# Earlier sends of turned blocks, one read back instead of three, later stores and a new VectorE price in a fused attention and feed-forward kernel

## The chip, the cores and the metric

The kernel runs on one core of one Trainium2 chip. The metric is the device time of one execution in microseconds (us); a measurement is the median of several executions. The core's engines are PE (matrix products; PEld is its weight load), DVE (VectorE), ACT (ScalarE), POOL (GpSimd) and SP (SyncE, which here only issues DMAs). Each engine works through its own instructions in program order and waits on semaphores for the others.

## What is computed

All in fp32, for 2048 tokens of 576 numbers, 32 heads of 18, and a hidden width of 4608:

```python
x = A_x
xn = _layernorm(x, axis=-1)
return x + _A_ref(xn, A_wqkv, A_wo) + _B_ref(xn, B_w1, B_w2)
```

`_A_ref` is attention in which a token looks at eight keys: itself and the tokens 2, 4, ... 14 before it; the result is multiplied by `wo`. `_B_ref` is `relu(xn @ w1) @ w2`. The kernel gets fp32 accuracy from a faster matmul format (fp32r) by splitting each operand into a high part and a rest (low part) and adding three products.

## The kernel before

**Phases and blocks.** The tokens are split by parity, since a step of 2 never leaves it: a phase (`ph`) holds the 1024 tokens of one parity as eight blocks of 128 (`i`), in pairs of 256 columns (`tb`). A phase runs over 12 chunks of w1/w2 (`c`), four `tb`, and three pieces of 128 hidden columns (`f`): 144 **slots** in a phase, 288 in all, numbered in that order (`slots`, L574). Slot n of the main loop (L867) has PE do half of a pair of first-layer products (`h_two`, L615, for slots two ahead; 14 pairs of matmuls in even slots, 13 in odd ones), then the second-layer products of the slot (`o_two`, L641). In odd slots ACT takes the relu into `hhi` and DVE makes the rest `hlo` (L597, L600). In slots with f = 2, `o_out` (L695) adds the four PSUM results into x on DVE (L709); in the last chunk the finished blocks are then stored by SP (L714). PSUM banks for the first layer alternate between two pools, except near q, k, v work, when only two banks serve, so that `h_two` of an even slot waits for `hlo` of the slot before.

**Attention** comes in four units of eight heads per phase. Eight slots in a row (7 to 14, 31 to 38, 55 to 62, 79 to 86 of a phase) also have the q, k, v products of one unit (`qkv_tile`, L406), which makes a slot 5.7 us instead of 3.1. The rest is DVE work, queued by `attention` (L449) in the slot after the unit's last block: products with the keys (`qk_mul`, L465), their sums (`qk_sum`, L468; after the last one POOL puts the mask in, L471), the softmax (`sm_max`, L477, to `sm_div`), products with the values (`av_mul`, L497) and their sums (`av_add`, L504).

**The plan.** While the program is written out, it keeps two estimated clocks, `t["pe"]` and `t["dve"]`. `dve(n)` (L133) prices a VectorE instruction of n elements at (n + 130) / 960 us. At the end of each slot `run_bg` (L522) takes pieces of attention from the queue as long as the DVE's clock with the next piece stays within `t["pe"] + margin(n)` (L859). So prices and margins decide in which slot each piece stands in DVE's program, and nothing else.

**wo.** In chunk 10, slots 122, 125, 128 and 131 of a phase (266, 269, ... in the second) also add the attention result times wo, two blocks each; such a slot lasts about 10 us. A block of attention output must be turned first: `wo_a` (L535) turns 32 x 32 tiles on DVE (L541, L542) into a tile `tr` (two buffers), `blocks_out` (L353) sends it to DRAM in four DMAs of 80 KB (L358), `wo_f` (L547) reads it back in one DMA of 320 KB with the blocks in place (L549; tile `xn`, three buffers), and `wo_s` (L551) splits it on ACT (L558) and DVE (L559, L560). The slots of these four steps come from `WO_STEPS`, counted from the block's slot: -5, -4, -3, -1 for even blocks and -4, -3, -2, -1 for odd ones.

**x of the second phase.** Its first four blocks go the same way between slots 126 and 143: load, `stats`, `norm_turned` (ACT), `xt_a` (turn, L373), `blocks_out`, `xt_f` (L377: three DMAs, one of 256 KB and two of 32 KB), `xt_s` (split, L391 to L395). `XT_STEPS` gives their slots, counted from 132. The normed block and its turned copy lie in one buffer of the attention products' pool `pr` (two buffers). The other four blocks are turned by PE. Slot 144 is the first whose `h_two` needs blocks 2 and 3.

**SP's queue.** SP issues in program order: within a slot first the staging loads of weights (`stage_more`, four splits ahead, five buffers `st`, so that a load waits for the split before the one it follows), then what `at` put there, then what `late` put there. A wait of SP for a transfer holds all later issues.

Of the kernel before, what the change touches and what calls it, by code (L numbers as in the profile page):

```python
# [10 lines left out]
F32 = mybir.dt.float32  # L11
# [7 lines left out]
P = 128  # L19
# [13 lines left out]
WO_CHUNK = 10  # L33

XT_STEPS = (
    (-6, 0, 1, 2, 3, 4, 7),
    (-5, 1, 2, 3, 4, 5, 8),
    (-3, 2, 3, 4, 5, 6, 10),
    (3, 4, 5, 6, 7, 8, 11),
)  # L40

WO_STEPS = ((-5, -4, -3, -1), (-4, -3, -2, -1))
HEADW = (-9, -8, -7, -6, -5, -4)
FIRST = 4

# [14 lines left out]
def tile_body(ctx: ExitStack, tc: tile.TileContext, x, wqkv, wo, w1, w2, out):  # L60
    nc = tc.nc
    S, D = x.shape
# [4 lines left out]
    NCH = NF // C  # L67
    KT = 4
    DR = D - KT * P
# [25 lines left out]
    turned = pool("turned", 4, space=bass.MemoryType.DRAM)  # L95
# [17 lines left out]
    o_v = out.rearrange("(p i two) d -> two i p d", i=NI, two=NPH)  # L113


    t = {"pe": 0.0, "dve": 0.0}
# [14 lines left out]
        return ins  # L131

    def dve(n):  # L133
        t["dve"] += (n + 130) / 960.0


    tasks = deque()
# [108 lines left out]
    X, XT, XN, MR = {}, {}, {}, {}  # L246
# [116 lines left out]
    def norm_turned(ph, i):  # L363
        nm, r = MR.pop((ph, i))
        z = prp.tile([P, W, UD], F32, name="pr").rearrange("p w c -> p (w c)")
        XN[ph, i] = xn, _ = z[:, 0:D], z[:, D : 2 * D]
        nc.scalar.activation(xn, X[ph, i], AF.Identity, bias=nm)
        nc.scalar.activation(xn, xn, AF.Copy, scale=r)

    def xt_a(ph, i):  # L370

        xn, tr = XN.pop((ph, i))
        nc.vector.transpose(tr, xn)  # L373
        dve(D)
        TD[ph, i] = turned.tile([D // 32, 32, P], F32, name="words"), tr

    def xt_f(ph, i):  # L377
        tb, h = divmod(i, 2)
        if h == 0:
            XT[ph, tb] = xtp.tile([P, 10, TBN], F32R, name="xT")  # L380
        z, td = f32(XT[ph, tb][:, 0:5, h * P : (h + 1) * P]), TD.pop((ph, i))[0]
        nc.sync.dma_start(z[:, 0:KT], td[0 : 4 * KT].rearrange("(k c) j i -> (c j) k i", k=KT))
        for rows in slice(0, DR), slice(DR, P):
            nc.sync.dma_start(z[rows, KT], td[4 * KT : D // 32].rearrange("c j i -> (c j) i"))

    def xt_s(ph, i):

# [11 lines left out]
    TD = {}  # L399
# [42 lines left out]
    bg = deque()  # L442
# [6 lines left out]
    def attention(ph, u):  # L449
        qo, k, v = QO[ph], KK[ph, u], VV[ph, u]  # L450
# [57 lines left out]
        n, big = NI * W * HG, W * UD  # L508
# [2 lines left out]
                for j in (i, i + 1):  # L511
                    bg.append((big, f, (j,)))
        for f in (sm_max, sm_sub, sm_exp, sm_sum, sm_rcp, sm_div):
            bg.append((0 if f is sm_exp else n + 130, f, ()))
        for i in range(0, NI, 2):
            for j in (i, i + 1):
                bg.append((big, av_mul, (j,)))
# [155 lines left out]
    def o_mm(n, out=True, which=range(2)):  # L673
# [18 lines left out]
        if out:  # L692
            o_out(n, which)

    def o_out(n, which=range(2), rows=False):  # L695
        ph, c, tb, f = slots[n]
        if f < C - 1:
            return
        end = n == len(slots) - 1
        t["dve"] = max(t["dve"], t["pe"] - 0.4)  # L700
        order = [(k, h) for k in which for h in range(2)]
        if rows:
            order.sort(key=lambda z: z[1])
        elif end:
            order.sort(key=lambda z: (z[0], -z[1]))
        for k, h in order:
            i = 2 * tb + k
            acc, cols = X[ph, i], CUT[h]
            nc.vector.tensor_tensor(acc[:, cols], PO[k, h], acc[:, cols], op=ALU.add)  # L709
            dve(cols.stop - cols.start)  # L710
            if end and k:
                (nc.scalar if h else nc.sync).dma_start(o_v[ph, i][:, cols], acc[:, cols])
            elif c == NCH - 1 and (k, h) in (order[-1], order[-2 if rows else 1]):
                nc.sync.dma_start(o_v[ph, i], acc)  # L714


    todo = {}
# [1 line left out]
    def at(n, f, *a):  # L719
        todo.setdefault(n, []).append((f, a))  # L720
# [3 lines left out]
    def late(n, f, *a):  # L724
        todo_late.setdefault(n, []).append((f, a))
# [3 lines left out]
    for ph in range(NPH):  # L729
# [7 lines left out]
        for u in range(NU):  # L737
            s = b + UNIT0 + u * UNIT_STEP
            plan.append((s - 5, wq_tasks, ((ph, u), u)))
            for i in range(NI):  # L740
                at(s + i, qkv_tile, ph, u, i)
                busy_m.add(s + i)
            late(s + NI + 1, attention, ph, u)
        plan.append((b + WO_CHUNK * SPC - 6, wo_tasks, (ph,)))
        for i in range(NI):
            z = b + WO_CHUNK * SPC + C * (i // 2) + C - 1
            turn, send, back, parts = (z + k for k in WO_STEPS[i % 2])
            late(turn, wo_a, ph, i)
            late(send, blocks_out, ph, i)
            (at if i % 2 else late)(back, wo_f, ph, i)  # L750
            at(parts, wo_s, ph, i)
        if ph + 1 < NPH:
            e = b + SPP - SPC
            for i in range(NI):
                if i >= len(XT_STEPS):
                    z = e + 3 + 2 * i - (i == NI - 1)
# [6 lines left out]
                load, first, second, turn, send, back, parts = (e + k for k in XT_STEPS[i])  # L763
# [77 lines left out]
    h4[0]()  # L841
    h4[1]()
    o_out(2, (0,))
    x4 = make_xt(0, 4, parts=True)
    for f in x4[:3]:
# [13 lines left out]
    def margin(n):  # L859

        odd, qkv = n % 2 == 0, n + 1 in busy_m
        due = sum(z[0] <= n + 1 for z in (*staged, *tasks))
        if slots[n][3] == 1:
            return (1.8 if odd else 2.7) + 2.4 * qkv - 0.8 * due
        return (2.5 if odd else 3.5) + 2.4 * qkv - 0.8 * due

    for n in range(FIRST, len(slots)):  # L867
        if n == ROW0:
# [47 lines left out]
```

## Time and profile before

| | us |
|---|---|
| time, median of 3 | 1172.0 (1169.96 to 1173.31) |
| the profiled execution's own time | 1171.2 |
| its span, first to last instruction | 1169.5 |
| PE busy in it | 1152.5 |
| DVE busy in it | 804.8 |
| mean granted clock of PE | 0.996 |

The span is what the trace covers; the profiled execution took 1.7 us more around it. All times of single instructions below are from that execution, in us from the start of the span. In rows of the timeline a merged group shows the start, the length and the count, and in brackets the idle time before it with what ended it. Rows of the waits show the sum, the number and the longest.

### The profile page before, as it was taken

What the parts mean: (1) busy time and instruction counts of PE and PEld (TensorE: products, weight loads), DVE (VectorE), ACT (ScalarE), POOL (GpSimd) and SP (SyncE); (2) the same over time, 40 slices, a digit from 0 to 9 for tenths busy, and PEclk for the clock granted to TensorE, in tenths of its full rate; (3) what the DMA queues carried; (4) which work ended last, traced back from release to release, by engine and by line L of the source; (5) the groups of instructions that cost most, each with busy time, mean ns of one, the idle gap of its engine ahead of it and who ended that gap; (6) DMA issues with size and microseconds to landing.
All of it is one profiled execution on the core that took longest, in us unless ns stands there. A gap on an engine that the chain in (4) does not pass through costs nothing.

```text
span 1169.5 us, 38344 instructions
## 1 busy us (share of the span) xinstructions
PE 1152.5 (99%) x17114; PEld 1142.7 (98%) x17114; DVE 804.8 (69%) x1457; ACT 287.7 (25%) x756; POOL 43.4 (4%) x60
## 2 busy tenths in 40 slices
PE   9999999999999999899999999999999999998998
PEld 8999999999999999899989999999999999998998
DVE  7428687878877888553663286977787878884533
ACT  5322222221222222121432122122222212221210
POOL 3200000000000000000010000000000000000000
PEclk9999999999999999999999999999999999999999
DMA  5312312311222212643552212122213222226502
GB/s 183 98 38 64 84 45 58 84 56 47 73 66 68 67 34 65 155 110 90 138 173 66 59 50 78 45 63 78 56 58 80 58 58 66 54 64 135 111 14 82
DMA packets 149940, 89.71 MB, mean 77 GB/s; under 512 B 58528, under 2 KB 133536, under 8 KB 149776
## 3 DMA queue, kind: packets, MB, share of 16 engines
q1 hardware_dynamic: 146816, 78.61, 25.5%
q10 hardware_dynamic: 2960, 8.65, 2.5%
q8 instruction: 135, 2.21, 0.8%
q14 instruction: 29, 0.24, 0.1%
HBM read 67.90 MB, written 11.14 MB: 68 GB/s over the span
## 4 chain that ended last, share of the span: by engine, by line
PE 93%; DMA 3%; SPq 1%; DVE 1%; ACT 1%; issue 1%; DVEq 0%; POOL 0%; ACTq 0%
PE po L129 40%; PE pm L129 27%; PE ph L129 22%; PE ph L119 1%; PE po L119 1%; DMA turned<-tr 1%; SPq L358 1%; DMA words<-pr 1%; DMA xn<-turned 1%; PE pm L303 1%; DVE x L709 0%; DMA xT<-words 0%; DMA x<-in_x 0%; DVE hlo L600 0%; SPq L179 0%
## 5 line engine op out<-in xcount | busy, mean ns | idle before, releaser
L129 PE MATMUL po<-w2t,hhi 64*128 64x256 f32 (+1 forms) x4448 | 450.5, 292 | 0.1
L129 PEld LDWEIGHTS po<-w2t,hhi 64*128 64x128 f32 x4448 | 365.0, 185 | 2.4 <-issue 1.2
L129 PE MATMUL po<-w2t,hlo 64*128 64x256 f32 (+1 forms) x2224 | 340.8, 290 | 0.0
L129 PE MATMUL ph<-xT,w1t 64*128 64x256 f32 x4698 | 303.4, 275 | 3.1 <-ACT xT L391 2.9
L129 PEld LDWEIGHTS ph<-xT,w1t 64*128 64x128 f32 x4698 | 291.0, 185 | 5.9 <-ACT xT L391 3.1
L709 DVE TENSOR_TENSOR x<-po,x 128x320 f32<-128x320 f32 (+1 forms) x384 | 149.7, 450 | 175.6 <-PE po L129 172.9
L129 PEld LDWEIGHTS po<-w2t,hlo 64*128 64x128 f32 x2224 | 224.3, 185 | 0.0
L129 PE MATMUL pm<-wq,xT 64*128 64x432 f32 x1728 | 180.6, 354 | 0.0
L129 PE MATMUL pm<-xT,w1t 64*128 64x256 f32 x2808 | 177.9, 273 | 0.0
L129 PEld LDWEIGHTS pm<-xT,w1t 64*128 64x128 f32 x2808 | 171.9, 184 | 0.0
L129 PEld LDWEIGHTS pm<-wq,xT 64*128 64x128 f32 x1728 | 162.5, 184 | 2.0
L597 ACT ACTIVATE hhi<-ph 128x256 fp32r<-128x256 f32 x183 | 60.8, 382 | 326.2 <-PE ph L129 294.2
L600 DVE SCALAR_TENSOR_TENSOR hlo<-ph,hhi 128x256 fp32r<-128x256 f32 x183 | 69.3, 417 | 75.6 <-ACT hhi L597 75.3
L597 ACT ACTIVATE hhi<-pm 128x256 fp32r<-128x256 f32 x105 | 34.7, 382 | 259.8 <-PE pm L129 259.3
L465 DVE TENSOR_TENSOR pr<-qo,k 128x1152 f32<-128x1152 f32 x64 | 84.9, 1350 | 2.0 <-DMA k<-k 2.0
L468 DVE TENSOR_REDUCE lg<-pr 128x64 f32<-128x1152 f32 x64 | 84.7, 1344 | 0.0
L497 DVE TENSOR_TENSOR pr<-lg,v 128x1152 f32<-128x1152 f32 x64 | 83.9, 1347 | 0.1
L434 ACT ACTIVATE k<-pm 128x144 f32<-128x144 f32 x64 | 19.3, 302 | 238.0 <-PE pm L129 191.1
L600 DVE SCALAR_TENSOR_TENSOR hlo<-pm,hhi 128x256 fp32r<-128x256 f32 x105 | 39.6, 418 | 44.3 <-ACT hhi L597 43.1
L504 DVE TENSOR_TENSOR pr<-pr 128x288 f32<-128x288 f32 (+1 forms) x128 | 69.7, 599 | 0.0
L166 DVE TENSOR_TENSOR w2t<-st,w2t 128x576 fp32r<-128x576 f32 x72 | 53.9, 749 | 16.2 <-ACT w2t L162 16.2
L166 DVE TENSOR_TENSOR w1t<-st,w1t 128x640 fp32r<-128x640 f32 x70 | 56.9, 812 | 2.2 <-ACT w1t L162 1.3
(87 smaller groups left out, 706.3 us busy)
## 6 DMA issues: line engine op xcount, KB each, us to landing
st<-in_w SPq DMA_DIRECT2D x72, 288.0 KB, 2.9
st<-in_w SPq DMA_DIRECT2D x72, 256.0 KB, 3.0
st<-in_wqkv SPq DMA_DIRECT2D x32, 216.0 KB, 3.1
turned<-tr SPq DMA_DIRECT2D x64, 80.0 KB, 2.9
xn<-turned SPq DMA_DIRECT2D x16, 320.0 KB, 3.3
st<-in_w SPq DMA_DIRECT2D x144, 32.0 KB, 2.7
out<-x SPq DMA_DIRECT2D x15, 288.0 KB, 2.5
x<-in_x SPq DMA_DIRECT2D x14, 288.0 KB, 4.1
```

The source lines that it names most:

```text
L119: nc.tensor.matmul(o, l, r, start=start, stop=stop)
L129: ins = nc.tensor.matmul(o, l[z], r[z], start=start, stop=stop)
L166: nc.vector.tensor_tensor(lo, src, f32(hi), op=ALU.subtract)
L303: nc.tensor.transpose(pa[:, k, :], src[:, k * P : (k + 1) * P], ident)
L434: nc.scalar.activation(k[:, W - 1 + j, :], pq[:, 1, :], AF.Copy)
L465: nc.vector.tensor_tensor(pr[i], q, window(k, i), op=ALU.mult)
L468: nc.vector.tensor_reduce(lg[:, i], pr.pop(i).rearrange(heads, d=Dh), axis=AX.X, op=ALU.add)
L497: nc.vector.tensor_tensor(pr[i].rearrange(heads, d=Dh), e, window(v, i).rearrange(heads, d=Dh), op=ALU.mult)
L504: nc.vector.tensor_tensor(o, z[:, 0:n], z[:, n : 2 * n], op=ALU.add)
L597: nc.scalar.activation(hi, pt, AF.Relu)
L600: nc.vector.scalar_tensor_tensor(lo, pt, 0.0, f32(hi), op0=ALU.max, op1=ALU.subtract)
L709: nc.vector.tensor_tensor(acc[:, cols], PO[k, h], acc[:, cols], op=ALU.add)
```

## The change

The steps in slots are new for the first four blocks of the second phase's x: read back later, and for the fourth block everything but the last step one slot later (the read back two). A block for wo is turned seven slots ahead of its products, the even one of a pair sent at the next slot's `at`, the odd one at its `late`; both are read back two slots ahead and split one ahead. The first blocks of x are turned in three instructions, the last 64 columns twice, so that the DRAM tile has the form of wo's and one DMA reads it back. Stores of the last chunk are issued in the slot after the adds. The price of a VectorE instruction in the plan is (n + 70) / 960, with 520 more for the softmax's two reductions instead of 130 for each softmax step, and the margin before a slot with q, k, v is 0.8 smaller after even slots.

```diff
 XT_STEPS = (
-    (-6, 0, 1, 2, 3, 4, 7),
-    (-5, 1, 2, 3, 4, 5, 8),
-    (-3, 2, 3, 4, 5, 6, 10),
-    (3, 4, 5, 6, 7, 8, 11),
+    (-6, 0, 1, 2, 3, 5, 7),
+    (-5, 1, 2, 3, 4, 6, 8),
+    (-3, 2, 3, 4, 5, 7, 10),
+    (4, 5, 6, 7, 8, 10, 11),
 )
-WO_STEPS = ((-5, -4, -3, -1), (-4, -3, -2, -1))
+WO_TURN = -7
...
     def dve(n):
-        t["dve"] += (n + 130) / 960.0
+        t["dve"] += (n + 70) / 960.0
...
-        XN[ph, i] = xn, _ = z[:, 0:D], z[:, D : 2 * D]
+        XN[ph, i] = xn, _ = z[:, 0:D], z[:, 512:1152]
...
         xn, tr = XN.pop((ph, i))
-        nc.vector.transpose(tr, xn)
-        dve(D)
-        TD[ph, i] = turned.tile([D // 32, 32, P], F32, name="words"), tr
+        for k in range(2):
+            nc.vector.transpose(tr[:, 512 + k * DR : 512 + (k + 1) * DR], xn[:, 512:D])
+            dve(DR)
+        nc.vector.transpose(tr[:, 0:512], xn[:, 0:512])
+        dve(512)
+        TD[ph, i] = turned.tile([5 * 4, 32, P], F32, name="turned"), tr
...
-        nc.sync.dma_start(z[:, 0:KT], td[0 : 4 * KT].rearrange("(k c) j i -> (c j) k i", k=KT))
-        for rows in slice(0, DR), slice(DR, P):
-            nc.sync.dma_start(z[rows, KT], td[4 * KT : D // 32].rearrange("c j i -> (c j) i"))
+        nc.sync.dma_start(z, td.rearrange("(k c) j i -> (c j) k i", k=5))
...
-            bg.append((0 if f is sm_exp else n + 130, f, ()))
+            bg.append((0 if f is sm_exp else n + 520 if f in (sm_max, sm_sum) else n + 70, f, ()))
...
+    def store(ph, i):
+        nc.sync.dma_start(o_v[ph, i], X[ph, i])
+
...
-            elif c == NCH - 1 and (k, h) in (order[-1], order[-2 if rows else 1]):
-                nc.sync.dma_start(o_v[ph, i], acc)
+            elif end and h == 0:
+                store(ph, i)
+            elif c == NCH - 1 and h == 1 and not end:
+                at(n + 1, store, ph, i)
...
-            turn, send, back, parts = (z + k for k in WO_STEPS[i % 2])
+            turn = z + WO_TURN
             late(turn, wo_a, ph, i)
-            late(send, blocks_out, ph, i)
-            (at if i % 2 else late)(back, wo_f, ph, i)
-            at(parts, wo_s, ph, i)
+            (late if i % 2 else at)(turn + 1, blocks_out, ph, i)
+            at(z - 2, wo_f, ph, i)
+            at(z - 1, wo_s, ph, i)
...
         if slots[n][3] == 1:
-            return (1.8 if odd else 2.7) + 2.4 * qkv - 0.8 * due
-        return (2.5 if odd else 3.5) + 2.4 * qkv - 0.8 * due
+            return (1.8 if odd else 2.7 + 2.4 * qkv) - 0.8 * due + 1.6 * (odd and qkv)
+        return (2.5 if odd else 3.5 + 2.4 * qkv) - 0.8 * due + 1.6 * (odd and qkv)
```

## The prediction

> **What bounds the kernel now.** I read the page's busy rows first, then the view of what PE waited for, then the lengths of single slots, and last the queues around the long ones.
>
> ```profile
> PE 1152.5 (99%) x17114; PEld 1142.7 (98%) x17114; DVE 804.8 (69%) x1457; ACT 287.7 (25%) x756; POOL 43.4 (4%) x60
> ```
>
> PE is the bound: 1152.5 us of 1169.5. No part of the change takes a matmul away, so all there is to win is time in which PE stood or ran slowly.
>
> ```profile
> PE po L129 <- ACT k L558: 7.5, 2, 4.0
> PE ph L129 <- ACT xT L391: 2.9, 1, 2.9
> ```
>
> These are PE's two large waits: twice for the turned blocks of wo's first products (L558), once for the turned x of the second parity (L391). Their price is more than the wait. I take a slot from its first matmul of the first layer to the next slot's, and ask the view of stretches for single slots (columns: stretch and length, PE, PEld, DVE, ACT, POOL busy, granted clock, DMA share, GB/s):
>
> ```profile
> 135.21:153.19 17.98, 17.98 (x238) 17.48 (x236) 12.32 (x19) 4.85 (x14) 2.86 (x3) 1.00 0.17 51
> 153.19:170.41 17.22, 17.22 (x239) 17.20 (x236) 14.82 (x27) 4.21 (x16) 0.00 (x0) 1.00 0.23 58
> 484.66:500.71 16.05, 12.03 (x164) 11.82 (x162) 3.57 (x8) 0.74 (x1) 0.00 (x0) 0.89 0.51 105
> 507.07:517.22 10.15, 10.15 (x163) 10.15 (x160) 4.19 (x11) 1.29 (x3) 0.00 (x0) 1.00 0.48 88
> 1065.68:1081.14 15.46, 11.95 (x165) 11.74 (x163) 3.62 (x8) 1.46 (x2) 0.00 (x0) 0.89 0.55 113
> 569.12:573.34 4.22, 4.09 (x57) 3.63 (x55) 2.78 (x9) 0.18 (x1) 0.75 (x2) 1.00 0.46 71
> 576.44:579.65 3.21, 3.21 (x56) 3.21 (x54) 3.12 (x7) 3.01 (x8) 0.00 (x0) 1.00 0.64 87
> 589.04:598.16 9.12, 6.24 (x61) 5.20 (x59) 4.91 (x11) 2.88 (x7) 0.00 (x0) 0.81 0.90 299
> 601.25:605.35 4.10, 4.10 (x62) 3.78 (x59) 1.86 (x5) 1.63 (x4) 0.00 (x0) 1.00 0.28 81
> ```
>
> Slot 122 (484.66) lasts 16.05 us where the next slot with wo, 125, lasts 10.15: 5.9 lost, of which 4.0 is waiting and the rest a clock of 0.89 behind it. Slot 266 (1065.68) loses 5.3. Slot 144 (589.04) lasts 9.12 against 4.10 for slot 146, which has the same work: 5.0. Slot 138 (569.12) loses 1.0 against slot 140. Slots 31 to 33 together last 17.98 against 17.22 for 34 to 36: 0.76. That last loss comes six times, in the chain of waits from the first to the last of these rows, where the usual piece of 28 takes 1.6:
>
> ```profile
> 141.14 2.24 PE ph L129 x28
> ...
> 164.86 1.62 PE ph L129 x28
> ...
> 915.82 2.20 PE ph L129 x28
> ```
>
> So 4.6 (six units), 6.0 (x, slots 138 and 144) and 11.2 (wo) are within reach, 21.8 us in all.
>
> **Part 1: the plan's clock and margins.** The DVE's rows in order of time (start, length):
>
> ```profile
> 133.78 1.35 DVE L465 TENSOR_TENSOR pr<-qo,k 128x1152 f32<-128x1152 f32 x1
> 135.05 2.60 DVE L468 TENSOR_REDUCE lg<-pr 128x64 f32<-128x1152 f32 x2
> 138.87 1.15 DVE L477 TENSOR_REDUCE m<-lg 128x64 f32<-128x512 f32 x1 [1.21 <-POOL lg L471]
> ...
> 140.67 0.75 DVE L600 SCALAR_TENSOR_TENSOR hlo<-ph,hhi 128x256 fp32r<-128x256 f32 x2
> ```
>
> An instruction is recorded for 1.35 us, but the next starts after 1.27, which is (1152 + 70) / 960: the new constant is what the engine does start to start, the old one (130) was 0.06 too dear each. The reductions of the softmax, dearer than their length, now get 520 + 70: (512 + 590) / 960 = 1.15, the recorded L477. So the engine is not overbooked by the cheaper price. I worked the rule of run_bg and margin through, slot by slot, with both sets of constants: attention goes out one or two pieces earlier and no more, since a piece of 1.27 either fits under the slot's bound or doesn't.
>
> In before, slot 30 holds a qk_mul (133.78), two qk_sum and sm_max; sm_max waits 1.21 for POOL, and so hlo of slot 31 ends at 141.4, while slot 32 wanted its PSUM bank at 141.1. That is the 0.76. After, the last qk_sum goes out in slot 29, and slot 30 holds sm_max and sm_sub: qk_sum ends near 134.6, POOL's mask 135.8, sm_max and sm_sub 137.5, slot 31's split 138.2, hlo 138.9: two us before the need. What is late next? The slots with q, k, v are packed denser, and attention is done in slot 36 instead of 38. Start to start, slot 31 puts 11 instructions of 7.9 us on DVE and slot 32 nine of 4.3 (four of them adds that wait for PE until 146.4); from 137.5 that is 145.4 and 149.7, and with slot 33's split and hlo 151.1. Slot 34 wants the bank at 152.5: 1.4 to spare, and slot 36 has more. I count **4.0** of the 4.6; bounds 0 (something else holds hlo) and 4.6.
>
> [...]
>
> **Part 2: wo's turned blocks.** SP's queue, and the DVE beside it:
>
> ```profile
> 471.82 0.38 SPq L174 DMA_DIRECT2D st<-in_w  x1
> ...
> 472.81 0.59 SPq L179 DMA_DIRECT2D st<-in_w  x1
> 474.16 0.39 SPq L174 DMA_DIRECT2D st<-in_w  x1
> ...
> 476.28 2.27 SPq L358 DMA_DIRECT2D turned<-tr  x4
> 478.65 0.48 SPq L190 DMA_DIRECT2D st<-in_w  x1
> 480.34 0.38 SPq L549 DMA_DIRECT2D xn<-turned  x1
> ...
> 487.00 0.38 SPq L549 DMA_DIRECT2D xn<-turned  x1
> ...
> 1061.58 3.74 SPq L358 DMA_DIRECT2D turned<-tr  x4
> ```
> ```profile
> 487.00 3.11 DMA xn<-turned
> 490.12 0.74 ACT k L558
> 490.91 10.07 PE po L129 x123
> ```
> ```profile
> 465.03 0.76 DVE L600 SCALAR_TENSOR_TENSOR hlo<-ph,hhi 128x256 fp32r<-128x256 f32 x2 [0.58 <-ACT hhi L597]
> ...
> 466.66 0.75 DVE L166 TENSOR_TENSOR v<-st,wq 128x576 fp32r<-128x576 f32 x1
> ...
> 472.38 0.77 DVE L541 STREAM_TRANSPOSE tr<-qo 128x576 f32<-128x576 f32 x1
> ```
>
> Block 1's read back (487.00) is what PE waits for: 3.11 to land, 0.74 on ACT, matmul at 490.91; PE had been ready 4.0 before. The change turns blocks 0 and 1 after slot 115 (two turns, 1.7 us, 465.8 to 467.5) and sends them in 116. But SP issues in program order, and between these sends and the reads back of slot 120 now stand the sends of blocks 2 and 3 too (turned after 118, sent in 119), and all staging loads of slots 117 to 120. Following SP: its w1 load of slot 116 waits for the subtract that was at 466.66, now about 468.2. From there a w1 load takes 1.6 (471.82 to 473.40) to 2.1 (474.16 to 476.28), a send 2.3, a w2 load 0.5, a read back 0.4. Ahead of block 1's read back stand four w1 loads (6.4 to 8.4), four sends (9.2), three w2 loads (1.5) and block 0's read back (0.4): 17.5 to 19.5, so it is issued at 485.7 to 487.7, against 487.00. Before, only two sends stood there, but SP spent some 4 us waiting for them to land. PE starts at 489.6 to 491.6: a gain of 1.3 or a loss of 0.7. I take 0.3 for the first phase, 0.2 for the second, which was shorter by 0.5: **0.5**; the wait of PE stays. The w2 load of slot 117, now behind two sends, comes late to ACT's split of slot 119 and may hold slot 120 up to 1.4 us; this comes out of the same wait of slot 122 and costs nothing as long as that is there. There is one new wait: tr has two buffers, so the turns of blocks 2 and 3 stand on DVE until the sends of 0 and 1 have landed, about 477, and behind them the split and hlo of slot 119; that is the same up to 1.4. Blocks 4 to 7 have a slot of 10 us ahead of them, and cost nothing.
>
> **Part 3: x of the second parity.**
>
> ```profile
> 567.84 2.91 SPq L358 DMA_DIRECT2D words<-pr  x4
> ...
> 574.72 2.20 SPq L358 DMA_DIRECT2D words<-pr  x4
> ...
> 582.29 2.39 SPq L358 DMA_DIRECT2D words<-pr  x4
> ```
> ```profile
> 584.04 4.27 DMA words<-pr
> 588.45 3.04 DMA xT<-words
> ```
> ```profile
> 568.64 0.78 DVE L267 BATCH_NORM_STATS2 bst<-x 128x6 f32<-128x288 f32 x2
> ...
> 570.43 1.54 DVE L709 TENSOR_TENSOR x<-po,x 128x256 f32<-128x256 f32 x4
> ```
>
> Before, each read back stands right behind its own send. SP waits there for the landing, and the next send comes after it: 567.84, 574.72, 582.29 are the sends of blocks 1, 2 and 3, nearly 7 us apart, and block 3's read back leaves at 588.45. After, the next block's send stands between a send and its read back, three reads become one, and the stores go behind the sends. Following SP with a send at 2.2, a load or store at 0.5 and a read at 0.4: send of block 0 at 562.1 as before, two stores, block 1's send at 565.2, block 3's load at 567.5 (its buffer is free once block 0's store has landed, by 567), block 0 read back at 568.0, block 2's send at 569.0 when its turn is done, blocks 1 and 2 read back at 571.7 and 574. Block 3's own steps stand a slot later in the plan: its load lands near 571.5, statistics until 572.6, ACT's norm until 575.1, and its turn is on DVE behind slot 139's split, hlo and block 0's parts, to 579.0. Its send leaves then, lands at 583.3 to 585.6 (4.27 in the row above), and the read back follows, 3 to 5 us ahead of 588.45. The wait was 2.9. With the clock behind it slot 144 gets 4.5 of its 5.0. Slot 138: block 3's statistics (568.64) stood ahead of the adds (570.43) that PE wanted; they now stand a slot later, 0.9 of 1.0. The extra small transposes cost four times 0.3 us of DVE that is waiting there. **5.4**; bounds 2.5 and 6.0. Stores in the last chunk a slot later: no PE work waits for them, 0.
>
> [...]
>
> **Sum.** 4.0 + 0.5 + 5.4 = 9.9 from the profiled 1171.2 (span 1169.5 and 1.7 around it): 1161.3; the median shown is 0.8 higher, so I say 1162.
>
> **Rivals.**
> *Reads back in time.* If the sends issue faster than these rows show, block 1 is there at 486.9 in both phases: the whole 11.2 goes, 1171.2 - 4.0 - 5.4 - 11.2 = 1150.6. For it: seven slots are 22 us. Against: SP's sum of 17.5 at the least.
> *The unit stall stays.* For it: it hangs on one slot's packing, and POOL's mask stays in the chain. Against: two us to spare. 1161.3 + 4.0 = 1165.
> *The DVE is as slow as recorded.* By 0.075 more for each of some 23 instructions, hlo of slot 33 is 0.4 late and that of 35 0.6: 1 us six times, 1167. [...]
> *The sends pile up* (the other side). Eight sends close together, all on the DMA engines with the loads: at 1061.58 four of these transfers took SP 3.74 instead of 2.27. If all four ahead of the read back cost that, and the w1 loads 2.1, block 1 comes 5.9 + 0.7 us later, twice 6.6: 1171.2 - 9.4 + 13.2 = 1175. It turns slower than before when a send costs over 2.27 + (4.7 - 0.7) / 4 = 3.3 us. Against: the DMA engines were busy 0.51 of slot 122, and a send at 2.27 or so is the commoner row.
>
> **How the numbers follow.** Forecast 0.58, full gain 0.07, unit stall stays 0.16, slow DVE 0.06, pile-up 0.13, half of it beyond 1175. A measurement here tells about 0.3% (3.5 us) from no change: under 1168.5 is faster. Faster 0.87, same 0.06, slower 0.07. The range takes the forecast with the bounds of its parts and the two cases above it, and leaves out the full gain and the pile-up: 1155 to 1168.5.
>
> **What the profile would show.** Right: slots 31 to 33 at 17.2 and no PEld wait for hlo; slot 138 near 3.3 and slot 144 near 4.6, with no wait of ACT for xT's transfer; the four sends of wo in two pairs from about 470, the reads back at 485.7 to 487.7, and PE still waiting 2 to 4 us for L558's successor. Wrong: reads back before 483, slot 34 or 36 longer than 5.8, or a new wait of PE for the adds in slot 120 that is longer than what slot 122 gives back.

## The result, and the profile after

The changed kernel takes 1179.8 us (median of 4, 1178.9 to 1182.3); the kernel before took 1171.3 beside it. The ratio is 1.0075, 95% interval 1.0052 to 1.0097: slower by 8.5 us, where 9.9 less was forecast. The profiled execution took 1182.3 (span 1180.4), the longest of the four, so the terms below add up to about 11 and not to 8.5.

From the page of the changed kernel, and from the view of what PE waited for:

```profile
PE 1157.4 (98%) x17114; PEld 1145.2 (97%) x17114; DVE 806.2 (68%) x1465; ACT 288.9 (24%) x756; POOL 45.0 (4%) x60
```
```profile
PE po L128 <- ACT k L558: 7.7, 4, 3.6
PE po L128 <- DVE x L712: 5.8, 3, 2.2
PE ph L128 <- ACT xT L391: 1.7, 1, 1.7
```

PE has the same instructions. The wait for wo's blocks (L558) is as long as before; the wait for x (L391) is 1.2 shorter; a new one, for the adds into x (L712), costs 5.8. Slot by slot, first from before (slots 66, 120, 141), then from after (slots 31 to 33 together, then 66, 120, 122, 266, 138, 140, 141, 144; columns as in the prediction):

```profile
287.89:291.06 3.17, 3.17 (x56) 3.17 (x54) 3.17 (x7) 0.00 (x0) 0.00 (x0) 1.00 0.01 3
478.43:481.60 3.17, 3.17 (x57) 3.17 (x54) 3.17 (x8) 0.00 (x0) 0.00 (x0) 1.00 0.76 159
579.65:582.72 3.07, 3.07 (x54) 3.07 (x52) 2.97 (x9) 1.28 (x3) 0.00 (x0) 1.00 0.96 346
```
```profile
135.92:153.26 17.34, 17.34 (x238) 17.34 (x236) 16.29 (x26) 4.98 (x14) 2.65 (x3) 1.00 0.22 57
287.36:291.45 4.09, 4.09 (x57) 3.63 (x54) 4.09 (x9) 0.00 (x0) 0.00 (x0) 1.00 0.01 2
478.92:484.69 5.77, 4.13 (x57) 3.66 (x54) 4.44 (x12) 1.80 (x4) 0.00 (x0) 1.00 0.99 253
487.79:504.82 17.03, 13.32 (x165) 12.83 (x163) 4.41 (x10) 1.47 (x2) 0.00 (x0) 0.80 0.55 119
1074.86:1092.04 17.18, 13.16 (x164) 12.66 (x162) 4.41 (x10) 1.47 (x2) 0.00 (x0) 0.80 0.55 119
572.98:576.22 3.24, 3.24 (x56) 3.24 (x54) 1.89 (x6) 0.00 (x0) 0.00 (x0) 1.00 0.68 118
579.32:583.78 4.46, 3.77 (x56) 3.35 (x54) 2.64 (x7) 3.98 (x9) 0.00 (x0) 1.00 0.92 288
583.78:590.88 7.10, 4.87 (x55) 4.50 (x52) 6.30 (x14) 4.23 (x10) 0.00 (x0) 0.80 0.81 206
597.53:603.98 6.45, 4.75 (x62) 4.00 (x59) 4.42 (x10) 2.88 (x7) 0.00 (x0) 1.00 0.42 133
```

Taking the slot starts of both traces in this way for all slots, the difference falls into groups: the six units (slots 31 to 33 and their like) -3.9; the three slots in which a unit's attention begins (16 to 18, 64 to 66 and their like) +3.0; slots 115 to 121 and 259 to 265 +5.8, nearly all in 120 and 264; slots 122 and 266 +2.7; slots 138 to 144 +2.0; the rest, no slot over 0.2, +1.6. So each part of the change did something that the prediction didn't have. These are two single executions: the slots in which PE stops longest (122, 266, 144) also differ by 1 to 2 us between kernels whose order around them is the same, as the experiments show.

**Around wo.** SP's queue, ACT's and PE's rows in order of time:

```profile
470.05 6.22 SPq L357 DMA_DIRECT2D turned<-tr  x8
476.37 0.94 SPq L189 DMA_DIRECT2D st<-in_w  x2
...
481.55 5.39 SPq L357 DMA_DIRECT2D turned<-tr  x8
...
488.79 1.10 SPq L549 DMA_DIRECT2D xn<-turned  x2
```
```profile
479.73 0.69 ACT L161 ACTIVATE w2t<-st 128x576 fp32r<-128x576 f32 x1 [6.58 <-DMA st<-in_w]
...
492.41 0.74 ACT L558 ACTIVATE k<-xn 128x640 fp32r<-128x640 f32 x1 [5.33 <-DMA xn<-turned]
```
```profile
482.35 0.74 PE L128 MATMUL po<-w2t,hhi 64*128 64x256 f32 x4 [1.64 <-DVE x L712]
...
493.20 0.58 PE L128 MATMUL po<-wq,k 64*128 64x256 f32 x1 [3.28 <-ACT k L558]
```

Two sends in a row hold SP for 6.22 and 5.39 us, so a block costs 3.1 and 2.7, not 2.3. The w2 load stands behind the first pair and leaves at 476.37. ACT has stood 6.58 for it when it splits it at 479.73; behind this split in ACT's program stands the relu, behind that on DVE `hlo` and then the adds, and slot 120's products wait for the adds. The reads back leave behind the second pair, at 488.8 to 489.9, and PE's first product with wo starts at 493.20 instead of 490.91.

**The second parity's x.** SP's queue, then what SP waited for, then DVE, ACT and PE, and from the chain that ended last the landing of two reads back (blocks 1 and 3):

```profile
568.16 1.01 SPq L696 DMA_DIRECT2D out<-x  x2
569.28 3.88 SPq L357 DMA_DIRECT2D turned<-pr  x4
573.25 0.45 SPq L254 DMA_DIRECT2D x<-in_x  x1
573.81 0.38 SPq L384 DMA_DIRECT2D xT<-turned  x1
574.28 3.78 SPq L357 DMA_DIRECT2D turned<-pr  x4
...
586.97 2.74 SPq L357 DMA_DIRECT2D turned<-pr  x4
```
```profile
SPq L254 <- DMA out<-x: 5.3, 2, 4.0
```
```profile
577.39 0.82 DVE L266 BATCH_NORM_STATS2 bst<-x 128x6 f32<-128x288 f32 x2 [2.52 <-DMA x<-in_x]
```
```profile
578.80 0.78 ACT L366 ACTIVATE pr<-x,nm 128x576 f32<-128x576 f32 x1 [6.53 <-DMA turned<-pr]
```
```profile
587.66 0.96 PE L128 MATMUL po<-w2t,hhi 64*128 64x256 f32 x4 [2.23 <-DVE x L712]
```
```profile
578.66 6.70 DMA xT<-turned
...
592.76 6.04 DMA xT<-turned
```

The store leaves at 568.16, behind it block 1's send, and only then block 3's load (573.25), into the buffer that the store frees. DVE's statistics wait for the load, ACT's norm for the statistics and for the send of block 1, and the splits and adds of slots 139 to 141 stand behind them on both engines. In slot 141 the last of it is block 1's read back: it leaves at 578.66, behind two sends of 3.88 and 3.78 us, lands 6.70 later, and ACT's split of it, DVE's and the adds follow. SP itself also stood 4.0 us before another load of x, for the store ahead of it; block 3's send came after that, at 586.97. Slot 138 starts at 572.98 here and at 569.12 before, so in before's time this send left at 583.1, and the read back (592.76) at 588.9: where it had been (588.45). It then took 6.04 to land, where the read of 256 KB took 3.04 before. Slot 144 is shorter all the same, since PE comes to it 4.6 us later, counted from slot 138.

### The profile page after: what moved, and what is told of

Its sections match the earlier page's. It is cut to its first block, busy times and chain, and to the rows that moved or that the text cites. A ratio compares the mean times of both kernels' runs of the same rounds, so it can differ in the third digit from the quotient of the medians.

```text
span 1180.4 us, 38310 instructions
## 1 busy us (share of the span) xinstructions
PE 1157.4 (98%) x17114; PEld 1145.2 (97%) x17114; DVE 806.2 (68%) x1465; ACT 288.9 (24%) x756; POOL 45.0 (4%) x60
## 4 chain that ended last, share of the span: by engine, by line
PE 91%; DMA 3%; SPq 2%; DVE 2%; ACT 1%; issue 1%; POOL 0%; DVEq 0%; ACTq 0%
PE po L128 40%; PE pm L128 27%; PE ph L128 22%; SPq L357 2%; DMA xT<-turned 1%; PE ph L118 1%; PE po L118 1%; DMA st<-in_w 1%; DMA xn<-turned 1%; PE pm L302 0%; DVE x L712 0%; DVE hlo L600 0%; DMA x<-in_x 0%; SPq L177 0%; DVE bst L266 0%
## 5 line engine op out<-in xcount | busy, mean ns | idle before, releaser
L128 PE MATMUL po<-w2t,hhi 64*128 64x256 f32 (+1 forms) x4448 | 456.4, 294 | 6.1 <-DVE x L712 5.8
L128 PEld LDWEIGHTS po<-w2t,hhi 64*128 64x128 f32 x4448 | 369.6, 185 | 10.9 <-ACT w2t L161 3.9
L128 PE MATMUL po<-w2t,hlo 64*128 64x256 f32 (+1 forms) x2224 | 345.3, 291 | 0.4 <-DVE hlo L600 0.4
L712 DVE TENSOR_TENSOR x<-po,x 128x320 f32<-128x320 f32 (+1 forms) x384 | 149.5, 449 | 186.2 <-PE po L128 183.3
L128 PEld LDWEIGHTS po<-w2t,hlo 64*128 64x128 f32 x2224 | 228.7, 186 | 0.6 <-DVE hlo L600 0.6
L128 PEld LDWEIGHTS pm<-wq,xT 64*128 64x128 f32 x1728 | 159.9, 184 | 3.6
```

Source lines behind the costliest of these rows:

```text
L128: ins = nc.tensor.matmul(o, l[z], r[z], start=start, stop=stop)
```

## The experiments

All times are medians beside runs of the kernel before on the same chip; the ratio in brackets is to that, with its 95% interval.

### One part of the change at a time

*Wo's steps put back*, all else as changed:

```diff
-WO_TURN = -7
+WO_STEPS = ((-5, -4, -3, -1), (-4, -3, -2, -1))
...
```

> The changed kernel with the four steps of wo's blocks (turn, send, read back, split) put back to where they were before; all else as changed. Theory (SP's queue around wo costs 8.2 us: slot 120 +2.6 and slot 264 +2.9 for a late w2 load, slots 122 and 266 +1.0 and +1.7 for a later read back): 1179.8 - 8.2 = 1171.6. Rival (the denser attention or the later phase as a whole makes these slots long, not the wo steps): stays at 1177 or more.

1174.2 (1.0016 to 1.0040): 5.6 less than the changed kernel. Slots 120 and 264 fell back to 3.17, which is the 5.5. Slot 266 fell to 15.46, but slot 122 went to 18.21, and that is no effect of the change: the kernel with x alone (below), which is the same as before up to there, has 18.32. With the old wo steps PE's longest wait in slot 122 is 4.0 to 5.0 in these traces, and slots 122 and 266 together last 31.5 to 35.2 in five of them; with the change's steps they last 34.2 in the changed kernel and 29.8 in the one with stores at once (below). So the +2.7 in these two slots isn't shown to come from the change. PE waits 7.7 for L558 in them, 7.5 before; the rest is the granted clock, 0.80 for 0.89.

*The plan alone*, put into the kernel before (price, softmax prices, margins):

```diff
-        t["dve"] += (n + 130) / 960.0
+        t["dve"] += (n + 70) / 960.0
...
-            bg.append((0 if f is sm_exp else n + 130, f, ()))
+            bg.append((0 if f is sm_exp else n + 520 if f in (sm_max, sm_sum) else n + 70, f, ()))
...
-            return (1.8 if odd else 2.7) + 2.4 * qkv - 0.8 * due
+            return (1.8 if odd else 2.7 + 2.4 * qkv) - 0.8 * due + 1.6 * (odd and qkv)
```

> The kernel before with only the plan's new VectorE price, softmax prices and margins. Theory (six units gain 3.9; four first slots of a unit lose 2.7 because the plan now puts four pieces where three stood and does not know that the first waits for a transfer of the key halo): 1171.3 - 1.2 = 1170.1, with slots 32, 56, 80 and their like 0.5 to 0.6 shorter and slots 18, 66, 186, 210 0.4 to 1.0 longer. Rival (those four losses come from elsewhere in the change): 1171.3 - 4 = 1167.3, and no loss in these slots.

1171.9 (0.9997 to 1.0017). The six units gain 4.0, the slots where attention begins lose 3.1. As the theory had it: the part is worth nothing as it stands.

*x alone*, put into the kernel before (steps, one read back, later stores); of its diff, which is that of the change:

```diff
-    (3, 4, 5, 6, 7, 8, 11),
+    (4, 5, 6, 7, 8, 10, 11),
...
+        nc.sync.dma_start(z, td.rearrange("(k c) j i -> (c j) k i", k=5))
...
+                at(n + 1, store, ph, i)
```

> The kernel before with only the change's part on x of the second parity: the new steps, the small transposes twice and one read back, stores a slot later. Theory (stores a slot later keep block 3's x buffer, and the sends, back to back, cost 3.8 us instead of 2.2, so that what slot 144 wins is lost in slots 140 and 141): slots 138 to 144 about as long in sum as before, up to 2 more; 1171 to 1173. Rival (the recorded prediction's working: this part alone wins 5.4, and only the other parts spoil it): 1166.

1172.4 (1.0006 to 1.0027), 2.1 more than before. Slots 138 to 144 together last 29.26, against 29.04 before. The predicted 5.4 isn't there, with nothing else changed.

Of the medians, the plan alone costs 1.2 (within what can't be told from nothing), x alone 2.1, and wo's steps 5.6: 8.9 together, where the whole change costs 8.5.

### The first slots of a unit

*The plan with one line more*, on the kernel of the plan alone:

```diff
         pr = {}
+        t["dve"] = max(t["dve"], t["pe"] - 1.2)
```

> The kernel before with the plan's new price, softmax prices and margins, and one line more: when a unit's attention is queued, the estimated VectorE clock is raised to at least 1.2 us before PE's, because the first product waits for the key halo. Theory (the four long first slots come from pieces planned into that wait): slots 18, 66, 186 and 210 fall back to 3.2, 2.8 us less than the plan alone, 1171.9 - 2.8 = 1169.1, if the units keep their 3.9. Rival (something else makes those slots long, or packing the pieces later brings the stall of slots 32, 56, 80 back): 1171 to 1173.

1168.7 (0.9969 to 0.9994). VectorE around slot 64 to 66, in the changed kernel and with the line:

```profile
282.82 2.63 DVE L465 TENSOR_TENSOR pr<-qo,k 128x1152 f32<-128x1152 f32 x2 [0.18 <-DMA k<-k]
285.36 2.61 DVE L468 TENSOR_REDUCE lg<-pr 128x64 f32<-128x1152 f32 x2
287.89 0.74 DVE L600 SCALAR_TENSOR_TENSOR hlo<-pm,hhi 128x256 fp32r<-128x256 f32 x2
288.55 1.54 DVE L712 TENSOR_TENSOR x<-po,x 128x256 f32<-128x256 f32 x4
```
```profile
282.08 2.63 DVE L466 TENSOR_TENSOR pr<-qo,k 128x1152 f32<-128x1152 f32 x2 [0.47 <-DMA k<-k]
285.70 0.76 DVE L601 SCALAR_TENSOR_TENSOR hlo<-pm,hhi 128x256 fp32r<-128x256 f32 x2 [0.99 <-ACT hhi L598]
```

The first product of a unit waits for the halo of the keys. The plan doesn't know that; with the lower price it put four pieces of 1.27 behind that wait, hlo and the adds came at 287.89 and 288.55, and slot 66 waited. With the line two pieces stand there, the four long slots are 3.17 again, and the units keep their gain (4.2). So the missing wait in the plan, and not the price, was the cost.

### The sends: queue, engine or packets

*Sends from ACT's queue*, at the same places:

```diff
-    def blocks_out(ph, i):
+    def blocks_out(ph, i, q=None):
...
-            nc.sync.dma_start(
+            (q or nc.sync).dma_start(
...
-            (late if i % 2 else at)(turn + 1, blocks_out, ph, i)
+            (late if i % 2 else at)(turn + 1, blocks_out, ph, i, nc.scalar)
```

> The changed kernel with wo's sends issued from ACT's queue instead of SP's, at the same places of the program. Theory (SP's program order is what costs: while SP issues sends at 0.7 us each, no load and no read back leaves): the w2 load of slot 117 and the reads back leave in time, slots 120 and 264 fall back to about 3.2 and slots 122 and 266 to 10 to 12, so 1179.8 - 5.5 - 9 to 13 = 1161 to 1165. Rival (the sends are slow in the DMA engines, packets of 128 bytes, and block everything whoever issues them): slots 122 and 266 stay at 16 or more, 1176 to 1180. A second rival (ACT is held by issuing eight DMAs, hhi comes late): the sum of slots 116 to 120 grows by 3 or more while slot 122 shrinks, about 1172.

1178.8 (1.0053 to 1.0084): no gain. ACT's rows:

```profile
467.19 6.79 ACTq L357 DMA_DIRECT2D turned<-tr  x8
...
481.97 8.14 ACTq L357 DMA_DIRECT2D turned<-tr  x7
...
491.28 1.36 ACT L558 ACTIVATE k<-xn 128x640 fp32r<-128x640 f32 x2
```

Whoever issues two blocks is held, SP 5.4 and 6.2 us, ACT 6.8 and 8.1. Slot 120 went back to 3.20 and slots 118 and 119 took its place (5.42 and 4.43), as the second rival said; slot 122 stayed at 15.49, as ACT came to the split of wo's blocks only behind the sends of the next pair, at 491.28. The theory that SP's order alone costs the time fell here.

*Wide packets*: the same bytes and the same number of DMAs, written in order, in packets of 512 bytes or more.

```diff
-                td[:, :, rows].rearrange("g j i -> j g i"),
-                tr[rows, :].rearrange("j (g i) -> j g i", i=32),
+                td[5 * r : 5 * r + 5].rearrange("g j i -> (g j) i").rearrange("(a b) i -> a b i", b=5),
+                tr[rows, :].rearrange("j (b i) -> j b i", i=P),
```

> The changed kernel with every send of a turned block (wo's and x's) writing the same 80 KB in the same number of DMAs, but in order, in packets of 512 bytes or more instead of 128. It leaves out the placing of the 32 x 32 tiles, so its attention and its second parity's normed x are not the reference's; the work of all engines is otherwise the same. Theory (a send costs 2.3 to 4.3 us because the DMA engines need that long for 2560 packets of 128 bytes, and moving them to ACT's queue therefore only moved the wait): sends fall to about 1.6 to 2 us of SP each, slots 120 and 264 to about 3.2, slots 122 and 266 by several us: -5.5 for the first two, -4 to -12 for the last two, so 1162 to 1170. Rival (it is SP's issue, about 0.57 us for each of the four DMAs, whatever the packets): sends stay at 2.3 or more, the time at 1177 to 1180.

1170.7 (0.9986 to 1.0010), 9.1 less than the changed kernel. SP's rows:

```profile
468.96 3.83 SPq L357 DMA_DIRECT2D turned<-tr  x8
...
479.11 3.65 SPq L357 DMA_DIRECT2D turned<-tr  x8
...
485.88 1.10 SPq L549 DMA_DIRECT2D xn<-turned  x2
```

Two blocks now hold SP 3.83 and 3.65 instead of 6.22 and 5.39; slot 120 is 4.23, slot 264 3.69, and slots 138 to 144 take 25.44 instead of 31.00. Slot 122 stays at 16.50, since the reads back are still behind the second pair. So a third to two fifths of the time that a send holds SP goes with packets of 128 bytes in scattered places (from 464 to 492 the changed kernel has 10816 packets under 512 bytes, this one 592; from issue to landing a DMA of a send takes 3.3 us there and 2.7 here, by the medians). SP's times differ by factors of 1.62 and 1.48, but what one packet costs can't be read from that: with wide packets a DMA of a send holds SP for 0.48 and 0.46 us on average, where the changed kernel's loads in that time have 0.39 to 0.59, so the 3.83 and 3.65 may be issuing alone.

*Reads back first*, in the changed kernel:

```diff
-            at(z - 2, wo_f, ph, i)
+            at(z - (3 if i < 2 else 2), wo_f, ph, i)
```

> The changed kernel with one number changed: wo's blocks 0 and 1 are read back three slots ahead of their products instead of two, so that both reads stand in SP's queue ahead of the sends of blocks 2 and 3. Theory (the queue's order keeps the read back late): reads back leave at about 481, PE waits no more in slots 122 and 266 (17.0 and 17.2 to about 11), slots 120 and 264 keep their +2.6 and +2.9, so 1179.8 - 12 = 1168. Rival (PE waits for the sends' landing or for the split, not for the queue): 1176 to 1180.

1166.0 (0.9942 to 0.9971), 13.8 less than the changed kernel for one number. SP's queue and slot 122:

```profile
481.03 0.95 SPq L549 DMA_DIRECT2D xn<-turned  x2
482.07 6.80 SPq L357 DMA_DIRECT2D turned<-tr  x8
```
```profile
487.07:497.33 10.26, 10.26 (x165) 10.26 (x163) 4.47 (x10) 0.54 (x1) 0.00 (x0) 1.00 0.76 127
```

The wait for wo is gone, though the sends cost as much (6.27 and 6.80 us for two blocks). So both hold: with packets of 128 bytes two blocks hold SP longer (6.22 and 5.39 us against 3.83 and 3.65), and the order decides what stands behind them. For slot 122 it is the order.

*One send a slot*, on the kernel with the plan and the halo line; the next pair keeps its old steps:

```diff
+WO_FIRST = ((-7, -6, -3, -1), (-7, -5, -2, -1))
...
-            turn, send, back, parts = (z + k for k in WO_STEPS[i % 2])
+            turn, send, back, parts = (z + k for k in (WO_STEPS if i > 1 else WO_FIRST)[i % 2])
...
-            (at if i % 2 else late)(back, wo_f, ph, i)
+            (at if i % 2 or i < 2 else late)(back, wo_f, ph, i)
```

> The kernel of the line on the halo, with one part more: blocks 0 and 1 of wo are turned seven slots ahead, sent at the ends of slots 116 and 117 (one each), read back in slots 119 and 120, ahead of any send of the next pair, which keeps its old steps. Theory (in the change it is the two sends of the next pair ahead of the reads back, and two sends in one slot ahead of the w2 load, that cost): the reads back leave before 481, slot 122 falls from 16 to 11 and slot 266 from 15.5 to 11, slot 120 stays near 3.2, so 9 to 11 less than that kernel, about 1159. Rival (the DMA engines are so full from slot 116 to 121 that an earlier send only delays the weights): slot 122 gains what slots 116 to 121 lose, within 2 of that kernel.

1160.4 (0.9907 to 0.9947), 8.2 less than its base. Slot 120 is 3.17, so the w2 load is in time with one send ahead of it; slots 122 and 266 are 13.7 and 13.2, not 11.

*Both reads in slot 119* asks for the rest of it:

```diff
-WO_FIRST = ((-7, -6, -3, -1), (-7, -5, -2, -1))
+WO_FIRST = ((-7, -6, -3, -1), (-7, -5, -3, -1))
```

> The kernel that sends wo's blocks 0 and 1 in slots 116 and 117, with one number changed: block 1 is read back in slot 119 too, right behind block 0, ahead of the w1 load of slot 120. Theory (an order in SP's queue in which both reads stand ahead of all that isn't needed sooner ends PE's wait): slots 122 and 266 fall from 13.7 and 13.2 to about 10.3, 1160.4 - 6.3 = 1154. Rival (the read's landing beside the next send on the DMA engines sets it): 1158 to 1161.

1158.5 (0.9883 to 0.9913): slots 122 and 266 at 12.4 and 11.6, not 10.3. Half right: PE still waits 0.6 and 0.7 for the two blocks in slot 122 and 0.8 in slot 266. The rival's reason, that the reads land beside other transfers, fits that, but nothing here shows it.

### x, one piece at a time

The base is the kernel of both reads in slot 119 (1158.5; slots 138 to 144 last 26.58 in it).

*Stores a slot later.* Block 3's load must stand behind the store in SP's queue, so it goes from 3 to 4 with it.

```diff
-    (3, 4, 5, 6, 7, 8, 11),
+    (4, 4, 5, 6, 7, 8, 11),
...
-            elif c == NCH - 1 and (k, h) in (order[-1], order[-2 if rows else 1]):
-                nc.sync.dma_start(o_v[ph, i], acc)
+            elif end and h == 0:
+                store(ph, i)
+            elif c == NCH - 1 and h == 1 and not end:
+                at(n + 1, store, ph, i)
```

> The kernel that sends wo's blocks 0 and 1 in slots 116 and 117 and reads both back in 119 (1158.5), with the change's later stores alone: each store of the last chunk in the slot after its adds. Since block 3 of x is loaded into the buffer that block 0's store frees, its load has to move a slot back as well, behind that store; its statistics and the rest stay. Theory (this is what makes block 3 late): load, statistics and norm 4 to 5 us later, slots 138 to 144 2 to 5 us longer in sum, 1160.5 to 1163.5. Rival (the recorded working: no PE work waits for a store, and the load is back in time): 1158 to 1159.

1162.2 (0.9909 to 0.9939): 3.7 more than the base, 3.0 by the ratios, since the two were not measured side by side. DVE and PE:

```profile
568.15 0.82 DVE L268 BATCH_NORM_STATS2 bst<-x 128x6 f32<-128x288 f32 x2 [5.85 <-DMA x<-in_x]
```
```profile
570.53 1.03 PE L130 MATMUL po<-w2t,hhi 64*128 64x256 f32 x4 [5.26 <-DVE x L714]
```

The statistics wait 5.85 for the load, which now stands behind block 1's send; the adds stand behind the statistics, PE waits 5.26 for the adds, and slot 138 lasts 10.24. This is the price of the later store and of the load that has to follow it. The opposite test is the changed kernel with *stores in the slot of the adds*:

```diff
-                at(n + 1, store, ph, i)
+                store(ph, i)
```

> The changed kernel with the stores of the last chunk in the slot of the adds again, as before; all else as changed. Theory (the later store keeps block 3's x buffer, so its load leaves 5 us late and statistics, norm, hhi and adds of slots 139 to 141 follow late): slots 140 and 141 lose their +1.25 and +4.0, 1179.8 - 5.3 = 1174.5. Rival (the read back and block 3's steps a slot later do it, or the sends' own time): within 1 us of 1179.8.

1177.3 (1.0038 to 1.0072), 2.5 less. Slot 140 fell to 3.19 and slot 141 to 4.56, but slot 144 rose from 6.45 to 8.11, with nearly the same wait (1.9 for 1.7) and a granted clock of 0.79 for 1.00: half of what was expected.

*One read back for three*, with the small transposes, on old steps:

```diff
-        nc.vector.transpose(tr, xn)
-        dve(D)
...
+        for k in range(2):
+            nc.vector.transpose(tr[:, 512 + k * DR : 512 + (k + 1) * DR], xn[:, 512:D])
+            dve(DR)
+        nc.vector.transpose(tr[:, 0:512], xn[:, 0:512])
+        dve(512)
...
+        nc.sync.dma_start(z, td.rearrange("(k c) j i -> (c j) k i", k=5))
```

> The same base with the change's form of x's turned blocks alone: last 64 columns turned twice, one read back of 320 KB instead of three of 256, 32 and 32 KB; steps and stores as before the change. Theory (three reads cost SP 1.15 us more than one, in each of three rounds ahead of the last): block 3's read back leaves 2 to 3 us earlier, slot 144 falls from 6.9 to about 4.5, 1156. Rival (the read waits for its send's landing anyway, and a bigger read takes longer to land): 1158 to 1159.

1157.3 (0.9872 to 0.9901), against 0.9883 to 0.9913 for the base: no difference that can be told. Block 3's send starts at 573.24 instead of 576.16 and takes 4.52 instead of 2.33; the one read of 320 KB then lands 5.15 after its issue, where the read of 256 KB took 2.89, and slot 144 is 6.70 instead of 6.86. SP's time was saved; it was not what bound.

*The steps alone*, with three reads and stores at once:

```diff
-    (-6, 0, 1, 2, 3, 4, 7),
-    (-5, 1, 2, 3, 4, 5, 8),
-    (-3, 2, 3, 4, 5, 6, 10),
-    (3, 4, 5, 6, 7, 8, 11),
+    (-6, 0, 1, 2, 3, 5, 7),
+    (-5, 1, 2, 3, 4, 6, 8),
+    (-3, 2, 3, 4, 5, 7, 10),
+    (4, 5, 6, 7, 8, 10, 11),
```

> The same base with the change's steps for x alone (reads back a slot later, behind the next block's send; block 3 a slot later), three reads and stores in the slot of the adds. Theory (sends then stand back to back, cost 3.5 instead of 2.2 us, and block 3's own slot later cancels the gain): slot 138 0.9 shorter, slots 140 to 142 1 to 3 longer, slot 144 within 2 of 6.9; 1157 to 1160. Rival (the recorded working: sends no longer wait for each other's landing, 3 to 5 us gained for block 3): slot 144 at 4.5, slot 138 at 3.3, 1155.

1157.9 (0.9877 to 0.9906), again not to be told from the base: slot 138 0.96 less, slot 141 1.2 more, slot 144 0.4 less.

*x's first two blocks earlier*, and then *block 3's statistics at the end of slot 137* as well (the last two lines, in the second kernel alone):

```diff
-    (-6, 0, 1, 2, 3, 4, 7),
-    (-5, 1, 2, 3, 4, 5, 8),
-    (-3, 2, 3, 4, 5, 6, 10),
+    (-6, -5, -4, -3, -2, 4, 7),
+    (-5, -3, -2, -1, 0, 5, 8),
+    (-3, 1, 2, 3, 4, 6, 10),
...
-    (3, 4, 5, 6, 7, 8, 11),
+    (3, 5, 5, 6, 7, 8, 11),
```

> The same with x's blocks 0 and 1 normed, turned and sent in slots 127 to 132 and block 2's sent in 136, instead of all after 132; three reads back each, and stores in the slot of the adds, as before. Theory (what holds x is that four sends and their reads share SP and the DMA engines in eight short slots): slot 144 falls from about 7 to 9 to 4.5, 2.5 to 4.5 less than without. Rival (block 3's own chain, from the store that frees its buffer to its read back, sets slot 144): no gain, within 1.

> The same again, with the statistics and norm of x's block 3 at the end of slot 137 instead of 136 and 137. Theory (block 3's statistics stand on VectorE ahead of the adds that PE waits for in slot 138): slot 138 falls from 4.0 to 3.2, 0.8 less than without; 1150 to 1152. Rival (its turn then comes late and slot 144 gives the gain back): within 0.5 of the one without.

1154.4 (0.9849 to 0.9887) and 1153.5 (0.9838 to 0.9871), 4.1 and 5.0 less than the base. With two sends out of the eight short slots, slot 144 lasts 4.3 and PE has no wait for x left. Slot 138 fell to 3.17 in the first of the two already, so the second edit wasn't needed; the two can't be told apart. They are 16 and 17 us below the kernel before.

*One more on top* of the last one: one read back for x, as above, and wo's block 0 read back in slot 118.

```diff
-WO_FIRST = ((-7, -6, -3, -1), (-7, -5, -3, -1))
+WO_FIRST = ((-7, -6, -4, -1), (-7, -5, -3, -1))
```

> The fastest so far (1153.5: wo's first pair early and read back in slot 119, x's first two blocks early, block 3's statistics late) with one read back for x and wo's block 0 read back in slot 118. Theory (PE still waits 1.5 us in slots 122 and 266 because both reads and a w1 load share the DMA engines from 479.4 on; block 0's has landed before if it is read a slot ahead): slots 122 and 266 from 12.6 and 11.3 to 10.3 or 11, 1151 to 1152. Rival (block 1's read is the one that ends last): within 0.7 of 1153.5.

1153.9 (0.9842 to 0.9876): nothing more. Slots 122 and 266 are 12.3 and 12.1: reading block 0 earlier doesn't shorten them, as the rival had it.

## Why the prediction was wrong

*Part 1, 4.0 gained in the units: right, and incomplete.* The units gained 3.9, and slots 34 to 36 did not suffer. "Attention goes out one or two pieces earlier and no more" was right too, but it was applied to the slots with q, k, v alone. In the slot where a unit begins, one piece more behind the wait for the halo cost 3.0 in sum, which the prediction had nowhere. The rival that the DVE is as slow as recorded fell: by it the units would have grown.

*Part 2, 0.5 gained: wrong, by 6.* The steps around wo cost 5.6. Two steps of the prediction failed. First the price: "a send 2.3" was read from sends that stand alone; in pairs they took 3.1 and 2.7, 11.6 for the four instead of 9.2, and the reads back left at 488.8 to 489.9, not 485.7 to 487.7. Second, and larger: that the late w2 load "comes out of the same wait of slot 122 and costs nothing as long as that is there". The load's delay was seen, but cost 2.6 and 2.9 where 1.4 at most was allowed, and nothing came back: PE's waits for wo stayed at 7.7 in sum for 7.5, because the reads back slid by the same sends. A delay is paid out of a later wait only if what ends that wait stays where it was. The rival of the pile-up named the mechanism and the side; its point of 3.3 us a send was too high, since it had the w2 load at nothing. It was given too small a chance. (That SP spent some 4 us waiting for two sends to land is misread: from 468 to 488 the view of its waits has 1.7 for that. The sum doesn't use it.)

*Part 3, 5.4 gained: wrong, by 7.* "Stores in the last chunk a slot later: no PE work waits for them, 0" failed: the load of x goes into the store's buffer and moves behind the store and block 1's send, and SP waits for a store ahead of another load. Alone it costs 3.0 to 3.7. "A send at 2.2" failed here too: back to back they took 3.88 and 3.78, so block 1's read back, reckoned for 571.7, left at 574.8 in before's time, and with it came the new wait of slot 141. The working had block 3's send at 579.0; in the same time it left at 583.1, behind SP's wait of 4.0 for a store. "One read instead of three" was counted as SP time and is worth nothing measurable; its longer landing, 6.04 against 3.04 for the 256 KB, was not counted. Slot 138 gained 0.98, where 0.9 of 1.0 was forecast; but it gains as much with x's first blocks earlier and block 3's statistics where they were, so the reason given, those statistics, isn't shown to be the cause.

The sum of the profiled slots: -3.9 as foreseen, +3.0 beside it, +5.8 around wo's sends, +2.7 in slots 122 and 266 (clock, not shown to be the change's), +2.0 around x, +1.6 spread over other slots.

What stays open: what the spread 1.6 is. In the kernel with the plan alone the same slots show +0.8, with the halo line -0.3.

## What to carry to other kernels

When a DMA is moved forward in a queue, list all that now stands behind it, price it as it runs among its new neighbours, and ask of each thing behind it who waits. A buffer's release is a consumer: before a store is delayed, look for the load that goes into its buffer. A forecast wait may pay for another delay only if the event that ends it doesn't move with that delay.

## What the runs showed of the hardware

The clock's price for a stop isn't set by the stop's length alone. With a wait of 2.4 in slot 266 (sends one a slot) the granted clock of the slot was 1.00, and with 2.1 in slot 144 of the base for x too; yet in the kernel with stores at once a wait of 1.9 in slot 144 came with 0.79, and in the changed kernel 2.2 in slot 141 with 0.80. Taken in shorter stretches, the granted clock of these traces is either 1.00 or 0.50, and 0.50, but for the start and the end, for one or two stretches of 3.41 us at a time (before: one each from 490.82, 593.23 and 1071.09; after: two each from 492.43 and 1079.52, one from 588.00). Slot 122 before, with one; slot 122 of the changed kernel, with two:

```profile
490.82:494.24 3.42, 3.33 (x30) 3.33 (x32) 1.89 (x4) 0.04 (x1) 0.00 (x0) 0.50 0.40 89
```
```profile
492.43:495.84 3.41, 2.21 (x15) 1.92 (x17) 2.54 (x5) 1.46 (x2) 0.00 (x0) 0.50 0.03 6
495.84:499.25 3.41, 3.41 (x33) 3.41 (x31) 1.11 (x4) 0.00 (x0) 0.00 (x0) 0.50 0.59 93
```

At half clock PE loses, by an estimate from these rows, half of the time that it is busy in such a stretch: 1.7 us in the first row, 1.1 and 1.7 in the other two. The first row has 30 products, the stretch behind it, at full clock, 54. Slot 266 has one stretch before and two after as well, and 1.1 more in each of the two slots is most of their +2.7. The kernel with x alone, which has before's order there, also has two in slot 122. Where a stop falls among these stretches counts. Slot 144 with stores at once, and in the base for x (here counted on from the clock's first step in that trace, at 4.64):

```profile
592.96:596.37 3.41, 1.55 (x21) 1.29 (x22) 1.44 (x3) 1.82 (x4) 0.00 (x0) 1.00 0.30 93
596.37:599.79 3.42, 3.42 (x26) 2.81 (x26) 2.82 (x7) 1.06 (x3) 0.00 (x0) 0.50 0.43 153
```
```profile
581.49:584.90 3.41, 1.82 (x28) 1.58 (x25) 0.76 (x2) 0.79 (x3) 0.00 (x0) 1.00 0.65 205
584.90:588.32 3.42, 2.87 (x34) 2.35 (x36) 2.83 (x7) 1.81 (x5) 0.00 (x0) 1.00 0.97 307
```

In the first, the stop of 1.86 lies in one stretch, and the next runs at half clock. In the second, 2.1 is split into 1.59 and 0.55, and the clock stays. Counted so in all 18 profiles after the first 12 us, every stretch at full clock in which PE stood 1.85 us or more was followed by one at half clock, and none in which it stood under 1.29; between these it went either way. In the traces of before and after, PE stood 2.23 to 3.41 us in the six stretches ahead of a fall, and 1.82 at most in the others at full clock. This is a count and not an experiment.

PE needn't stand for a whole stretch: with stores at once it worked 1.55 us of the one ahead of the fall in slot 144. No run here settles what decides between 1.29 and 1.85.
